# Linear attention on one core: two output stores cut unevenly by partitions, and three more warm-up matmuls

## The chip, the cores and the metric

One Trainium2 chip, one core of it. The time is device microseconds of one execution, the median of several runs; the profile comes from one profiled execution. The cast: TensorE (PE, with its weight loads as PEld), VectorE (DVE), ScalarE (ACT), GpSimd (POOL), and SyncE (SP), which here does nothing but issue transfers. Sixteen DMA engines carry the transfers of the core.

## The reference

Linear attention with the feature map ELU + 1, for B = 1, H = 32 heads, S = 2048 positions, D = 128, all in bf16:

```python
phi_q = jnp.where(q > 0, q + 1, jnp.exp(q)) + 1e-6
phi_k = jnp.where(k > 0, k + 1, jnp.exp(k)) + 1e-6
kv  = jnp.einsum("bhsd,bhse->bhde", phi_k, v)
z   = jnp.einsum("bhsd->bhd", phi_k)
num = jnp.einsum("bhqd,bhde->bhqe", phi_q, kv)
den = jnp.einsum("bhqd,bhd->bhq", phi_q, z)[..., None] + 1e-6
return num / den
```

Each head reads 512 KB each of q, k and v and writes 512 KB. Over 32 heads that is 50.3 MB read and 16.8 MB written.

## The kernel before, in words

The kernel works head by head. A head's 2048 positions lie as 128 partitions of 16 neighbouring positions, so that each partition's part of a tensor is one stretch of 16 x 128 bf16 = 4096 bytes in DRAM (`rows`, L262). The 16 positions of a partition make 16 tiles of 128 x 128.

For each head: the feature map of k is split in two summands, min(exp k, 1) + 1e-6 (`emk_sb`: exponential on ScalarE at L328, the rest on VectorE at L334) and max(k, 0) (`rk_sb`, GpSimd, L330). TensorE sums both against v into a 128 x 128 matrix and a column of sums (`kv`, L342 to L358, into `kvz_ps`). q is transposed on TensorE in two halves of eight tiles (L373, into `x_ps`); its feature map is again two summands, `emq_sb` and `rq_sb` (L384 to L393). Then TensorE computes numerator and denominator in one (L411, L417, into `o_ps`), VectorE adds the epsilon and takes the reciprocal (L456, L460), and VectorE multiplies into `o_sb` (L432, L438); for the last three heads ScalarE takes part of the multiplication (L447).

**The order.** A small planner (`Plan`) holds every operation with its engine and a key; each engine's program is its operations sorted by key, and semaphores are set where an operation needs another engine's result or a free buffer. A key is a position in heads: `h + 0.7` is 0.7 of the way through head h. TensorE's middle heads are a hardware loop; the other engines' programs are written out.

**Transfers.** SP issues all loads (L320) and all stores (L472), in one order by key; only the first head's v is issued by ScalarE (L315). k, q and v have six buffers each (`NBI`), the output has ten (`NBO`). A load is issued when its buffer is free, some six heads ahead. A store of head h has the key h + 1 + 0.18 h (`late`, L476), so that stores fall behind their heads more and more: head 8's stands at 10.44, head 14's at 17.52. Each store is one DMA of 128 partitions by 4096 bytes, except for the last two heads, which are cut by tiles into two and three pieces (`PIECES`, L212). Each output buffer has a semaphore of its own, further pieces get further ones (`EXTRA`); each DMA adds 16 to its semaphore when it has landed. At the end SP waits for all the output semaphores (L149 to L152).

**The warm-up.** Before any data arrives, TensorE runs `warm(9)` (L296): nine matmuls of 128 x 512 on a tile of zeros, into three banks of `o_ps` that nobody reads. The first loads its weights (L288), the other eight keep them (L277).

```python
for n, c in (("k", NBI), ("q", NBI), ("v", NBI), ("o", NBO + 3), ("x", 1)):
    for i in range(c):
        dsems[(n, i)] = es.enter_context(nc.semaphore(f"s_{n}{i}"))
...
late = h + 1.0 + 0.18 * h
for n, (t0, t1) in enumerate(PIECES.get(h, ((0, NT),))):
    store(t0, t1, late + 0.01 * n, bo if n == 0 else NBO + EXTRA[h] + n - 1)
```

Of the kernel before, what the change touches and what calls it, by code (L numbers as in the profile page):

```python
# [11 lines left out]
def _ap(base: bass.AP, elem_offset: int, dims):  # L12
    return bass.AP(base.tensor, base.offset + elem_offset, [list(base.ap[0])] + [list(d) for d in dims])
# [162 lines left out]
def bass_standalone__linear_attn_elu__prompt_kernel(  # L176
# [8 lines left out]
    NT = 16  # L185
# [3 lines left out]
    NBI = 6  # L189
    NBO = 10  # L190
# [20 lines left out]

    PIECES = {NH - 2: ((0, 6), (6, NT)), NH - 1: ((0, 6), (6, 12), (12, NT))}  # L212
    EXTRA = {NH - 2: 0, NH - 1: 1}
    LOOP, TURNS = 3, 4

    qf = q.rearrange("b h s d -> (b h) s d")
# [2 lines left out]
    of = out.rearrange("b h s d -> (b h) s d")  # L219

    with ExitStack() as es:
        def sb(name, shape, dt):
            return es.enter_context(nc.sbuf_tensor(name, shape, dt))
# [14 lines left out]
        o_sb = sb("o_sb", [P, NBO, NT, D], bf16)  # L238
# [11 lines left out]
        def dma_sem(name):  # L250
            return dsems[name]

        for n, c in (("k", NBI), ("q", NBI), ("v", NBI), ("o", NBO + 3), ("x", 1)):
            for i in range(c):
                dsems[(n, i)] = es.enter_context(nc.semaphore(f"s_{n}{i}"))

        block = es.enter_context(nc.Block())
        pl = Plan()

        def rows(x, h):  # L260
            return x[h].rearrange("(p j) d -> p (j d)", j=NT)
# [7 lines left out]
               reads=[("id0",)], writes=[("ident",)])  # L269
# [5 lines left out]
        def mm_held(pe, out, lhsT, rhs, start, stop):  # L275

            return pe.add_instruction(mybir.InstMatmult(  # L277
                name=nc.get_next_instruction_name(), engine=mybir.EngineType.PE, ldweights=False,
                ins=[pe.lower_ap(rhs), pe.lower_ap(lhsT)], outs=[pe.lower_ap(out)], start_tensor_calc=start,
                stop_tensor_calc=stop, tile_size=(P, P), tile_position=(0, 0), bass_skip_group_check=True))  # L280

        def warm(n):

            def f(pe):
                for w in range(n):
                    o = o_ps[:, (2 + w % 3) * 512:(3 + w % 3) * 512]
                    w_sb, zeros = warm_sb[:, :], _ap(warm_sb[:, :], 0, [[0, 4], [1, P]])
                    last = mm_held(pe, o, w_sb, zeros, True, True) if w else pe.matmul(o, lhsT=w_sb, rhs=zeros, start=True, stop=True)  # L288
                return last
            return f  # L290
# [2 lines left out]

        pl.add("act", -9, lambda a: a.activation(rden_sb[:, 0, 0:1], warm_sb[:, 0:1], ACT.Exp), reads=[("warm",)],
               writes=[("rden", 0, 0)])
        pl.add("pe", -9, warm(9), reads=[("warm",)], writes=[("banko", 2), ("banko", 3), ("banko", 4)])  # L296

# [6 lines left out]
        for h in range(NH):  # L306
# [3 lines left out]
            bi, b2, b3, bo = h % NBI, h % 2, h % 3, h % NBO  # L310

            def load(name, buf, src, key, h=h, bi=bi):
# [4 lines left out]
                if name == "v":  # L317
# [11 lines left out]
                   reads=[("k", bi)], writes=[("ek", b2)])  # L329
            pl.add("pool", h, lambda g, bi=bi, b3=b3: g.tensor_scalar(rk_sb[:, b3, :], k_sb[:, bi, :], BIG, 0.0,  # L330
                                                                      op0=ALU.min, op1=ALU.max),
                   reads=[("k", bi)] + ([("emq", 1)] if h == 2 else []), writes=[("rk", b3), ("rkx", b3), ("phik", b3)])
            pl.add("dve", at("emk", -3 + 0.95),
                   lambda d, b2=b2, b3=b3: d.tensor_scalar(emk_sb[:, b3, :], ek_sb[:, b2, :], 1.0, EPS, op0=ALU.min, op1=ALU.add),  # L334
                   reads=[("ek", b2)], writes=[("emk", b3)])

            def added(x, b3=b3):
# [3 lines left out]
                reads=[("emk", b3), ("rkx", b3)] + ([("emq", (h - 1) % 3)] if h else []), writes=[("phik", b3)])  # L341

            def kv(pe, tiles, srcs, h=h, bi=bi, b3=b3):
                for j in tiles:
# [16 lines left out]
                   reads=[("emk", b3), ("rk", b3), ("v", bi), ("ones",), ("vones",)], writes=[("bankkv",)])  # L361
            pl.add("pe", at("kv", -1.2), lambda pe, kv=kv: kv(pe, ADD, (rk_sb,)), reads=[("phik", b3), ("v", bi)], writes=[("bankkv",)])
            pl.add("act", at("kvs", -0.95), lambda a, b3=b3: a.activation(kvs_sb[:, b3, 1:], kvz_ps[:, 1:NC], ACT.Copy),  # L363
                   reads=[("bankkv",)], writes=[("kvs", b3)])
            pl.add("dve", at("zs", -1 + 0.905), lambda d, b3=b3: d.tensor_scalar(  # L365
                kvs_sb[:, b3, 0:1], kvz_ps[:, 0:1], kvz_ps[:, NC:NC + 1], None, op0=ALU.add),
                   reads=[("bankkv",)], writes=[("zs", b3)])
# [14 lines left out]
            for half in (0, 1):  # L382
                pl.add("act", h - 1.1 + 0.05 * half,
                       lambda a, b2=b2, c=cols(half): a.activation(eq_sb[:, b2, c], xT_ps[:, c], ACT.Exp),  # L384
                       reads=[("bankx", half)], writes=[("eq", b2, half)])
            pl.add("act", h - 1.0,
                   lambda a, b3=b3, c=cols(1): a.activation(rq_sb[:, b3, c], xT_ps[:, c], ACT.Relu),  # L387
                   reads=[("bankx", 1)], writes=[("rq", b3, 1)])
            pl.add("dve", at("rq", -2 + 0.948),
                   lambda d, b3=b3, c=cols(0): d.tensor_scalar(rq_sb[:, b3, c], xT_ps[:, c], 0.0, None, op0=ALU.max),  # L390
                   reads=[("bankx", 0)], writes=[("rq", b3, 0)])
            pl.add("dve", at("emq", -2 + 0.955),
                   lambda d, b2=b2, b3=b3: d.tensor_scalar(emq_sb[:, b3, :], eq_sb[:, b2, :], 1.0, EPS, op0=ALU.min, op1=ALU.add),  # L393
                   reads=[("eq", b2, 0), ("eq", b2, 1)], writes=[("emq", b3)])
# [4 lines left out]
            def nbank(b, h=h):  # L399
                return ("bankx", b) if h == NH - 1 and b < 2 else ("banko", b)  # L400
# [20 lines left out]
            for bank in range(NB):  # L421
                pl.add("pe", h + 0.7 + 0.001 * bank, num(bank), reads=phi,
                       writes=[nbank(bank)] + ([nbank(0)] if bank == 1 else []))
# [28 lines left out]
            for g, (b0, b1, place_d, runs) in enumerate(groups):  # L452
# [6 lines left out]
                    reads=banks, writes=[("den", b3, g)])  # L459
                pl.add("dve", key + 0.01, lambda d, b3=b3, b0=b0, b1=b1: d.reciprocal(  # L460
                    rden_sb[:, b3, 4 * b0:4 * b1], den_sb[:, b3, 4 * b0:4 * b1]),
                    reads=[("den", b3, g)], writes=[("rden", b3, g)])
                if g == 0:
                    pl.add("dve", h + 0.911, last_tile, reads=[nbank(0), nbank(1), ("rden", b3, 0)], writes=[("o", bo, NT - 1)])
                for n, (eng, t0, t1, *place_a) in enumerate(runs):
                    pl.add(eng, h + place_a[0] if eng == "act" else key + 0.012 + 0.004 * n,
                           div_act(t0, t1) if eng == "act" else div(t0, t1),
                           reads=[nbank(b) for b in range(t0 // 3, (t1 + 2) // 3)] + [("rden", b3, g)],
                           writes=[("o", bo, t) for t in range(t0, t1)])

            def store(t0, t1, key, slot, h=h, bo=bo):
                pl.add("sp", key, lambda sp: sp.dma_start(rows(of, h)[:, t0 * D:t1 * D],  # L472
                                                          o_sb[:, bo, t0:t1].rearrange("p j d -> p (j d)")),
                       reads=[("o", bo, t) for t in range(t0, t1)], dma=("o", slot))

            late = h + 1.0 + 0.18 * h  # L476
            for n, (t0, t1) in enumerate(PIECES.get(h, ((0, NT),))):
                store(t0, t1, late + 0.01 * n, bo if n == 0 else NBO + EXTRA[h] + n - 1)

# [29 lines left out]
```

## Time and profile before

| what | value |
|---|---|
| time, median of 3 runs (least to most) | 170.68 us (170.59 to 170.80) |
| the profiled execution's own time | 170.68 us |
| its span, first to last instruction | 168.8 us |
| mean granted TensorE clock | 0.994 |
| busy: PE, PEld, DVE, ACT, POOL | 94%, 90%, 89%, 93%, 62% of the span |
| HBM traffic over the span | 398 GB/s |
| a 512 KB load or store, issue to landing (median) | 13.2 to 13.8 us |
| the last store (128 KB), issue to landing | 4.0 us |

The profile is one page, drawn from a trace that can be queried. All its times are counted from the first instruction of the span; the execution's own time is 1.9 us longer than the span. The strip chart cuts the span into 40 slices of 4.2 us; a digit is the busy share in tenths, 9 meaning 90% or more. The chain of waits follows the work that ended last back to the start, each step to what released it. The trace also holds, for each DMA, the times at which its semaphore was raised, 16 times per DMA.

### The profile page before, as it was taken

The page shows a single profiled execution, that of the slowest core. Times are in us where ns is not written, and L with a number is a line of the kernel's source. Part 1 is how long each engine was busy: PE and PEld are TensorE (multiplying, and loading weights), DVE is VectorE, ACT ScalarE, POOL GpSimd, SP SyncE. Part 2 cuts the span into 40 slices and gives each one's busy share as a digit, 9 for nine tenths or more (in the row PEclk, how much of TensorE's full clock was granted, in tenths as well). Part 3 has the DMA queues.
Part 4 walks back from the last instruction along what each step waited for, and adds up shares of the span by engine and source line. Part 5 has one row for each costly group of instructions (what it writes and reads, how often), then busy time and mean ns, then how long its engine had stood idle before and what let it go on. Part 6 is the DMA issues. An engine that isn't in the chain of part 4 may idle for free.

```text
span 168.8 us, 6570 instructions
## 1 busy us (share of the span) xinstructions
PE 158.0 (94%) x3089; PEld 151.7 (90%) x2401; DVE 149.6 (89%) x293; ACT 157.3 (93%) x180; POOL 105.5 (62%) x72
## 2 busy tenths in 40 slices
PE   7588999999999999999999999999999999999940
PEld 0488999999999999999999999999999999999830
DVE  0144999999999999999999999999999999999870
ACT  4599999999999999999999999999999999996960
POOL 3836866666677776666667776666667776666000
PEclk9999999999999999999999999999999999999997
DMA  5999999999999999999999999999999999999982
GB/s 204 412 414 411 412 406 409 406 415 408 411 414 409 415 416 415 418 413 419 415 414 415 416 413 420 413 419 415 413 416 418 417 414 415 411 413 415 412 333 104
DMA packets 22848, 67.31 MB, mean 399 GB/s; under 512 B 2097, under 2 KB 2609, under 8 KB 22833
## 3 DMA queue, kind: packets, MB, share of 16 engines
q1 hardware_dynamic: 22688, 66.59, 98.5%
q10 hardware_dynamic: 144, 0.52, 0.8%
q8 instruction: 9, 0.15, 0.3%
q14 instruction: 7, 0.05, 0.1%
HBM read 50.33 MB, written 16.78 MB: 398 GB/s over the span
## 4 chain that ended last, share of the span: by engine, by line
PE 87%; DMA 3%; DVE 3%; ACT 3%; issue 0%; SPq 0%
PE kvz_ps L355 36%; PE o_ps L411 32%; PE x_ps L373 16%; DMA q_sb<-in_q_dram 3%; DVE o_sb L438 1%; PE o_ps L277 1%; ACT eq_sb L384 1%; PE o_ps L417 1%; PE kvz_ps L277 1%; ACT ek_sb L328 1%; ACT rq_sb L387 1%; DVE emk_sb L334 0%; DVE rden_sb L460 0%; DVE den_sb L456 0%; SPq L320 0%
## 5 line engine op out<-in xcount | busy, mean ns | idle before, releaser
L384 ACT ACTIVATE eq_sb<-x_ps 128x1024 bf16<-128x1024 bf16 x64 | 72.4, 1349 | 3.4 <-PE x_ps L373 3.4
L339 POOL TENSOR_TENSOR rk_sb<-rk_sb,emk_sb 128x640 bf16<-128x640 bf16 x32 | 44.7, 1396 | 47.4 <-DVE emq_sb L393 41.2
L328 ACT ACTIVATE ek_sb<-k_sb 128x2048 bf16<-128x2048 bf16 x32 | 72.2, 2256 | 1.7 <-DMA k_sb<-in_k_dram 1.7
L438 DVE TENSOR_TENSOR o_sb<-o_ps,rden_sb 128x768 bf16<-128x768 f32 (+2 forms) x63 | 68.0, 1119 | 0.1
L355 PE MATMUL kvz_ps<-v_sb,rk_sb 128*128 128x128 bf16 (+1 forms) x512 | 67.6, 218 | 0.0
L330 POOL TENSOR_SCALAR rk_sb<-k_sb 128x2048 bf16<-128x2048 bf16 x32 | 60.6, 1892 | 2.7 <-DMA k_sb<-in_k_dram 2.0
L411 PE MATMUL o_ps<-kvs_sb,emq_sb 128*128 128x129 bf16 x474 | 60.6, 220 | 0.3 <-DVE o_sb L438 0.3
L411 PE MATMUL o_ps<-kvs_sb,rq_sb 128*128 128x129 bf16 x474 | 60.6, 220 | 0.0
L355 PE MATMUL kvz_ps<-v_sb,emk_sb 128*128 128x128 bf16 (+1 forms) x352 | 55.4, 219 | 1.2 <-DVE kvs_sb L365 1.2
L277 PE MATMUL kvz_ps<-ones_sb,rk_sb 128*128 128x1 bf16 x388 | 53.3, 166 | 0.0
L355 PEld LDWEIGHTS kvz_ps<-v_sb,rk_sb 128*128 128x128 bf16 x512 | 47.0, 97 | 1.5
L411 PEld LDWEIGHTS o_ps<-kvs_sb,rq_sb 128*128 128x128 bf16 x474 | 46.2, 97 | 0.0
L411 PEld LDWEIGHTS o_ps<-kvs_sb,emq_sb 128*128 128x128 bf16 x474 | 45.4, 97 | 0.6 <-DVE o_sb L438 0.4
L387 ACT ACTIVATE rq_sb<-x_ps 128x1024 bf16<-128x1024 bf16 x32 | 43.7, 1366 | 0.0
L277 PE MATMUL kvz_ps<-ones_sb,emk_sb 128*128 128x1 bf16 x228 | 37.8, 167 | 0.0
L373 PE MATMUL x_ps<-ident,q_sb 128*128 128x128 bf16 x512 | 34.6, 222 | 1.7 <-DMA q_sb<-in_q_dram 1.7
L373 PEld LDWEIGHTS x_ps<-ident,q_sb 128*128 128x128 bf16 x512 | 30.6, 99 | 5.6 <-DMA q_sb<-in_q_dram 5.6
L355 PEld LDWEIGHTS kvz_ps<-v_sb,emk_sb 128*128 128x128 bf16 x352 | 33.9, 97 | 1.5 <-issue 1.5
L334 DVE TENSOR_SCALAR emk_sb<-ek_sb 128x2048 bf16<-128x2048 bf16 x32 | 21.8, 682 | 8.8 <-ACT ek_sb L328 8.8
L390 DVE TENSOR_SCALAR rq_sb<-x_ps 128x1024 bf16<-128x1024 bf16 x32 | 21.8, 680 | 2.5 <-ACT eq_sb L384 2.5
L393 DVE TENSOR_SCALAR emq_sb<-eq_sb 128x2048 bf16<-128x2048 bf16 x32 | 22.1, 691 | 0.4 <-ACT eq_sb L384 0.4
L363 ACT ACTIVATE kvs_sb<-kvz_ps 128x128 bf16<-128x128 f32 x32 | 20.3, 634 | 0.0
(39 smaller groups left out, 78.2 us busy)
## 6 DMA issues: line engine op xcount, KB each, us to landing
k_sb<-in_k_dram SPq DMA_DIRECT2D x32, 512.0 KB, 13.2
q_sb<-in_q_dram SPq DMA_DIRECT2D x32, 512.0 KB, 13.2
v_sb<-in_v_dram SPq DMA_DIRECT2D x31, 512.0 KB, 13.6
out_dram<-o_sb SPq DMA_DIRECT2D x30, 512.0 KB, 13.8
out_dram<-o_sb SPq DMA_DIRECT2D x3, 192.0 KB, 4.7
v_sb<-in_v_dram ACTq DMA_DIRECT2D x1, 512.0 KB, 4.4
out_dram<-o_sb SPq DMA_DIRECT2D x1, 320.0 KB, 5.6
out_dram<-o_sb SPq DMA_DIRECT2D x1, 128.0 KB, 4.0
```

The lines of the kernel that those rows point to most:

```text
L277: return pe.add_instruction(mybir.InstMatmult(name=nc.get_next_instruction_name(), engine=mybir.EngineType.PE, ldweights=False, ins=[pe.lo ...
L328: lambda a, bi=bi, b2=b2: a.activation(ek_sb[:, b2, :], k_sb[:, bi, :], ACT.Exp),
L330: pl.add("pool", h, lambda g, bi=bi, b3=b3: g.tensor_scalar(rk_sb[:, b3, :], k_sb[:, bi, :], BIG, 0.0, op0=ALU.min, op1=ALU.max), reads=[( ...
L334: lambda d, b2=b2, b3=b3: d.tensor_scalar(emk_sb[:, b3, :], ek_sb[:, b2, :], 1.0, EPS, op0=ALU.min, op1=ALU.add),
L339: pl.add("pool", h + 0.5, lambda g, added=added: g.tensor_tensor(out=added(rk_sb), in0=added(rk_sb), in1=added(emk_sb), op=ALU.add), reads ...
L355: last = pe.matmul(kvz_ps[:, 1 - l:NC + r], lhsT=w, rhs=rhs, start=first, stop=fin, skip_group_check=True)
L373: last = pe.transpose(xT_ps[:, j * P:(j + 1) * P], q_sb[:, bi, j * P:(j + 1) * P], ident[:])
L384: lambda a, b2=b2, c=cols(half): a.activation(eq_sb[:, b2, c], xT_ps[:, c], ACT.Exp),
L387: lambda a, b3=b3, c=cols(1): a.activation(rq_sb[:, b3, c], xT_ps[:, c], ACT.Relu),
L393: lambda d, b2=b2, b3=b3: d.tensor_scalar(emq_sb[:, b3, :], eq_sb[:, b2, :], 1.0, EPS, op0=ALU.min, op1=ALU.add),
L411: last = pe.matmul(o_ap, lhsT=x[:, b3, t * P:(t + 1) * P], rhs=kvs_sb[:, b3, :], start=first, stop=not first)
L438: return lambda d: d.tensor_tensor(out=o_sb[:, bo, t0:t1, :].rearrange("p (a b) d -> p a b d", b=n), in0=_ap(nfull(b), 512 * b + NC * (t0 ...
```

## The change

Two things. The stores of heads 8 and 14 are cut by partitions into three DMAs of 64, 63 and 1 partitions, one after the other in SP's order at the old place (keys `late`, `late + 0.01`, `late + 0.02`); the first keeps the buffer's semaphore, the others get four new ones. Rows and bytes stay as they were. SP issues four DMAs more, and its final wait covers four semaphores more. And the warm-up has twelve matmuls in place of nine. The order of all other instructions on all engines is unchanged.

```diff
+    UNEVEN = {8: (64, 63, 1), 14: (64, 63, 1)}
...
-        for n, c in (("k", NBI), ("q", NBI), ("v", NBI), ("o", NBO + 3), ("x", 1)):
+        for n, c in (("k", NBI), ("q", NBI), ("v", NBI), ("o", NBO + 7), ("x", 1)):
...
-        pl.add("pe", -9, warm(9), reads=[("warm",)], writes=[("banko", 2), ("banko", 3), ("banko", 4)])
+        pl.add("pe", -9, warm(12), reads=[("warm",)], writes=[("banko", 2), ("banko", 3), ("banko", 4)])
...
             late = h + 1.0 + 0.18 * h
+            if h in UNEVEN:
+                r0 = 0
+                for n, r in enumerate(UNEVEN[h]):
+                    pl.add("sp", late + 0.01 * n, lambda sp, h=h, bo=bo, r0=r0, r=r: sp.dma_start(
+                        rows(of, h)[r0:r0 + r, :], o_sb[r0:r0 + r, bo].rearrange("p j d -> p (j d)")),
+                        reads=[("o", bo, t) for t in range(NT)], dma=("o", bo if n == 0 else NBO + 2 + 2 * (h > 8) + n))
+                    r0 += r
+                continue
```

## The prediction, as recorded before the change was run

> **What bounds the kernel now.** I read the page from the top, then its chain of waits, and then, because two of them disagree, the last microseconds by windows and the sixteen completion events that the trace keeps of each transfer.
>
> ```profile
> span 168.8 us, 6570 instructions
> ...
> DMA  5999999999999999999999999999999999999982
> GB/s 204 412 414 411 412 406 409 406 415 408 411 414 409 415 416 415 418 413 419 415 414 415 416 413 420 413 419 415 413 416 418 417 414 415 411 413 415 412 333 104
> ...
> q1 hardware_dynamic: 22688, 66.59, 98.5%
> ...
> PE 87%; DMA 3%; DVE 3%; ACT 3%; issue 0%; SPq 0%
> ```
>
> The chain of waits is 87% TensorE. But the transfers run without a gap from the first slice to the last but two: 412 to 418 GB/s, and 98.5% of sixteen engines' span for SP's queue alone. Two resources are nearly full, so what counts is which of them ends last. The windows of the end tell (columns: stretch, its length, busy time of PE, PEld, DVE, ACT, POOL, granted clock, share of the 16 DMA engines, GB/s):
>
> ```profile
> core 0: us, PE busy (x) PEld busy (x) DVE busy (x) ACT busy (x) POOL busy (x), PEclk, DMA share, GB/s
> 163.00:164.50 1.50, 0.00 (x0) 0.00 (x0) 0.96 (x1) 0.88 (x3) 0.00 (x0) 1.00 0.75 290
> ...
> 165.50:166.00 0.50, 0.00 (x0) 0.00 (x0) 0.00 (x0) 0.00 (x0) 0.00 (x0) 1.00 0.62 222
> 166.00:166.50 0.50, 0.00 (x0) 0.00 (x0) 0.00 (x0) 0.00 (x0) 0.00 (x0) 1.00 0.13 50
> 166.50:167.00 0.50, 0.00 (x0) 0.00 (x0) 0.00 (x0) 0.00 (x0) 0.00 (x0) 0.87 0.11 38
> 167.00:167.60 0.60, 0.00 (x0) 0.00 (x0) 0.00 (x0) 0.00 (x0) 0.00 (x0) 0.50 0.07 25
> 167.60:168.20 0.60, 0.00 (x0) 0.00 (x0) 0.00 (x0) 0.00 (x0) 0.00 (x0) 0.50 0.03 12
> ```
>
> One engine of sixteen is a share of 0.06. From 166 us on two engines are at work, from 167 one. The last store's sixteen completion events say the same: the first fourteen at 166.12 to 166.4 us, the next at 167.24, the last at 168.34; the span ends at 168.82. Through the whole run the distance between the first and the last engine of a transfer grows: 0.24 us at the first load, 2.2 at 33 us, 3.1 at 128, 4.6 at 160. So one engine, which I call the late engine, has been behind all along and never idles; its work alone sets the end. It moves 25 GB/s even when it is alone (the row from 167.00), which is a sixteenth of the full rate: the other engines' rest does not speed it up. TensorE, VectorE and the last issue are some 2 us early for it:
>
> ```profile
> 163.01 0.96 DVE L438 TENSOR_TENSOR o_sb<-o_ps,rden_sb 128x768 bf16<-128x768 f32 x1
> ```
>
> **Price of a row.** 414 GB/s over 16 engines is 25.9 GB/s for one; a partition's row of a store is 4096 bytes, so 0.158 us. The 512 KB store gives each engine 8 of its 128 rows.
>
> **The uneven stores.** Bytes are the same. The 64 rows can go as 4 to each of 16 engines. For the 63 the trace has no example. What it does show in all its 131 DMAs is equal shares: the same number of rows to each engine taking part. 63 rows can be dealt in equal shares to 9, 7, 3 or 1 engines and to no larger number up to 16. The bounds: spread as evenly as can be (15 engines 4 rows, one 3): 0.0 us. All 63 on one engine: 4 + 63 = 67 rows in place of 8, 59 x 0.158 = 9.3 us a head, 18.6 for both. I take equal shares on the most engines, nine with 7 rows each, nearest to what the rows show. Then for each head nine engines get 4 + 7 = 11 rows (3 more), seven get 4 (4 fewer). Over both heads: nine engines +6 x 0.158 = **+0.95 us**, seven engines -8 x 0.158 = **-1.27 us**. The Trainium skill, page "DMA: Bandwidth & Descriptors", section "Why a DMA increments its semaphore by 16 and not by 1", states it as a rule: the largest number up to 16 that divides the slowest dimension, here nine, and always the lowest-numbered engines, so the same nine for both heads. By it the sum is the same; the sixteen events of each 128-row DMA agree with it, and no run here shows 63.
>
> The 1-row piece is one more row on one engine (0.158) or sixteen scraps of 256 bytes (about 0.01 each): 0 to 0.32 us for both; I take 0.03. Two more pieces a head bring each engine up to four completion writes of 6 ns, 0.02 us. The late engine also pays more than its share at stores: there four of its eight rows take 0.17 to 0.18 us, and it falls back about 0.12 us a store. With other rows this may be -0.24 to +0.34 for both heads; I take 0, the middle.
>
> Does it matter that the extra rows come at heads 8 and 14 and not at the end? The issues land 13 us later in the middle of the run, so every engine has a queue and an added row shifts all behind it. The loads can bear a lag of 0.95 us: k of head 31 lands at 145.80 and its exponential begins at 148.75; q lands at 150.98 for 154.7, v at 152.24 for 155.6. The four further issues on SP, and four waits more at its end (L149-152), lie under those 13 us and under the last landing. The ring of ten output buffers leaves head 18 to wait for head 8's last piece, issued 10.4 heads in: eight heads of cover.
>
> **The warm-up.** Three matmuls more of 128x512, on zeros.
>
> ```profile
> 1.39 3.62 PE L277 MATMUL o_ps<-warm_sb 128*128 128x512 bf16 x8
> 6.71 1.89 PE L373 MATMUL x_ps<-ident,q_sb 128*128 128x128 bf16 x16 [1.70 <-DMA q_sb<-in_q_dram]
> ...
> 9.70 0.15 PEld L355 LDWEIGHTS kvz_ps<-v_sb,emk_sb 128*128 128x128 bf16 x1
> 9.84 0.11 PEld L355 LDWEIGHTS kvz_ps<-v_sb,rk_sb 128*128 128x128 bf16 x1
> ```
>
> 3.62/8 = 0.45 each, 1.36 for three, so they end at 5.01 + 1.36 = 6.37, before q lands at 6.71: hidden, with 0.34 us of cover. If q came earlier than that it would cost the difference. They can also give something. Weight loads take 0.15 us up to 9.70 and 0.11 from 9.84: TensorE's clock goes up there. Were it up at 6.71, the first eight transposes (1.05 us on the chain) would take 1.05 x 0.11/0.15 = 0.77. So the gain is 0 to 0.3 us on the TensorE chain, and it ends there: that chain has 2 us to spare against the late engine, whose queue never empties. I count 0. The Trainium skill, page "TensorE: Matmul & The Clock Gate", section "What's actually happening", decides the clock over windows of some 3.4 us; counted back from 9.85 a window is 3.0 to 6.4, which the three matmuls fill, so by it the transposes would be fast; the sum is still 0.
>
> **Sum for the forecast.** Which engines are the nine decides the sign. By count alone the late engine is one of them 9 times in 16. Beside that: packets of different engines that start at one instant stand in the trace in one fixed order, hundreds of times without contradiction, and the late engine is fifth of sixteen. By the Trainium skill (the page and section above) the lowest nine are taken, which would include the fifth if that order is the engines' own; no view here gives an engine a number. So: late engine +0.95 + 0.03 + 0.02 = 1.0 us. It lands at 169.34, the span is 169.8. The profiled execution took 170.68 us, 1.9 beyond its span, and the median is 170.68 too: **171.7 us**, with 171.3 to 172.1 by the unknown terms (-0.4 to +0.4).
>
> **Rivals.**
>
> *Late engine relieved* (faster). If it is one of the seven, it lands at 168.34 - 1.27 = 167.07. The fourteen, nine of them fed 0.95 more, go from 166.4 to 167.35 at most, less what they idle at the end (0.75 of a share in the window from 163.00, so up to 0.4 us). If the second-last engine (167.24) is relieved too, or its late stay goes, the end is at 167.0 to 167.35: -1.0 to -1.3, **169.5 us**. For: 7 in 16. Against: the second-last stands thirteenth in that order, eight places from the late one; in a ring of sixteen, seven neighbours never hold both. But its delay is no store's: a 16 KB instruction fetch (1.1 us at 156.7) made it late, and a few more instructions may put that elsewhere. From the point where the late engine is among the seven, this decides. The Trainium skill, page "DMA: Bandwidth & Descriptors", section "Latency and other measured facts", has engines 7 and 15 as usually the slow ones: 15 would be relieved, 7 loaded.
>
> *Late one relieved, second-last loaded* (same): 167.24 + 0.95 = 168.19, 0.15 earlier: **170.5 us**. The same bin holds the case that the 63 rows are spread evenly and the change doesn't do what it says: 170.7.
>
> *All 63 on one engine* (much slower): +18.6 less the 2 us that an early engine has: about 187. Against it: no DMA of the trace is dealt so.
>
> **How the numbers follow.** Forecast 0.53; relieved 0.29; same 0.15; one engine 0.03. A measurement can tell about 0.2%, 0.34 us, from no change. Slower is 0.53 + 0.03 = 0.56, same 0.15, faster 0.29. The likeliest case's own range is 171.3 to 172.1; both signs hold much, so the range goes from 169.3 to 172.1 and leaves out the one-engine case and edges.
>
> **What would show it.** In the profile after, the landing of a 63-row piece must show nine data-bearing completion events; the late engine's last event minus the fourteen's should stay near 2 us or more for the forecast (all nine go up together) and fall to nothing for the rival. The DMA share after the fourteen end: one engine (0.06) is the forecast, several (0.3 or more) the rival. First transposes at 0.11 us a load, with kv starting at about 13.1 rather than 13.44, and no change at the end, show the warm-up. I am wrong if TensorE's end moves the span, or the late engine has no fixed place between runs.

## The result: 1.09 us slower, and the profile after

The changed kernel takes 171.72 us (median of 6 runs, 171.60 to 172.12), the kernel before 170.63 (170.47 to 170.80) in the same session: a ratio of 1.0067, 95% interval 1.0054 to 1.0080. The forecast was 171.7, on the slower side. The profiled execution took 171.6 us with a span of 169.7.

The page after, the same lines as of before:

```profile
span 169.7 us, 6581 instructions
...
DMA  5999999999999999999999999999999999999980
GB/s 209 406 418 414 406 409 408 390 416 416 405 415 411 416 416 415 418 412 418 415 416 416 416 415 418 415 417 417 416 414 418 417 416 413 413 417 413 405 328 34
...
q1 hardware_dynamic: 22708, 66.59, 98.1%
```

The bytes of SP's queue are the same, 66.59 MB, in 20 more packets, and the slices in the middle are as full as before. The difference is the last slice: 34 GB/s where it was 104. The windows of the end, with the columns of the prediction:

```profile
165.50:166.00 0.50, 0.00 (x0) 0.00 (x0) 0.00 (x0) 0.00 (x0) 0.00 (x0) 0.50 0.33 117
166.00:166.50 0.50, 0.00 (x0) 0.00 (x0) 0.00 (x0) 0.00 (x0) 0.00 (x0) 0.50 0.12 45
166.50:167.00 0.50, 0.00 (x0) 0.00 (x0) 0.00 (x0) 0.00 (x0) 0.00 (x0) 0.50 0.08 32
167.00:167.60 0.60, 0.00 (x0) 0.00 (x0) 0.00 (x0) 0.00 (x0) 0.00 (x0) 0.50 0.06 24
167.60:168.20 0.60, 0.00 (x0) 0.00 (x0) 0.00 (x0) 0.00 (x0) 0.00 (x0) 0.50 0.07 26
168.20:168.80 0.60, 0.00 (x0) 0.00 (x0) 0.00 (x0) 0.00 (x0) 0.00 (x0) 0.50 0.07 25
```

One engine (a share of 0.06 to 0.07) now works alone from 167 to 168.8; before, it was alone from 167.2 and done by 168. The last store's last event comes at 169.26 where it was 168.34, 2.9 us behind the fourteenth where it was 2.0. TensorE and VectorE are not later; their last multiply begins 0.25 us earlier than before:

```profile
162.76 0.96 DVE L439 TENSOR_TENSOR o_sb<-o_ps,rden_sb 128x768 bf16<-128x768 f32 x1
```

How the 63 rows are dealt can be read from the completion events of the pieces of 63 and 1 rows, one list for each DMA, in us:

```
head 8,  63 rows: 74.47 | 83.86 83.97 83.99 84.05 84.53 84.65 85.34 85.35 85.94
head 8,   1 row:  74.86 | 84.15
head 14, 63 rows: 109.83 | 118.29 118.45 118.56 118.91 118.95 119.76 119.78 119.79 121.17
head 14,  1 row:  110.16 | 118.75
```

The first event stands close to the issue, 9 us ahead of the others; a 128-row DMA has sixteen events and all at the landing. So nine engines carry the 63 rows and one carries the single row. The last event, 0.6 and 1.4 us behind the rest, is the late engine's.

How much later the late engine became takes care to read, for ahead of head 8 the last event of a transfer is not its own. It can be told by its habit: its event falls further back at each store, while the others keep their distances. The last four events of some stores, in us behind the store's first event (its landing in the first column); the late engine's are 2.01, 2.14, 2.28 and 2.41 before, 1.84, 3.02 and 3.17 after:

```
before  78.22 | 1.82 2.01 2.13 2.23      after  78.37 | 1.73 1.84 1.88 2.19
before  83.25 | 1.81 2.14 2.17 2.23
before  88.31 | 1.77 2.10 2.20 2.28      after  88.05 | 1.96 2.32 2.33 3.02
before  93.34 | 1.77 2.11 2.20 2.41      after  93.08 | 1.96 2.33 2.34 3.17
```

Ahead of head 8 its event is 0.02 us earlier than before (80.21 and 80.23), behind it 0.48 later (91.07 and 90.59), and at head 14 the difference goes from 0.51 to 1.01: two steps of 0.50, where the prediction had 0.475 for each. One further DMA a head on that engine, at the price of experiment 7, is the rest.

### The profile page after: what moved, and what is told of

It is laid out like the page before. It is cut to its first block, busy times and chain, and to the rows that moved or that the text cites. A ratio compares the mean times of both kernels' runs of the same rounds, so it can differ in the third digit from the quotient of the medians.

```text
span 169.7 us, 6581 instructions
## 1 busy us (share of the span) xinstructions
PE 157.2 (93%) x3092; PEld 150.4 (89%) x2401; DVE 149.9 (88%) x293; ACT 157.4 (93%) x180; POOL 105.6 (62%) x72
## 3 DMA queue, kind: packets, MB, share of 16 engines
q1 hardware_dynamic: 22708, 66.59, 98.1%
## 4 chain that ended last, share of the span: by engine, by line
PE 85%; ACT 5%; DMA 3%; DVE 3%; issue 1%; SPq 0%
PE kvz_ps L356 34%; PE o_ps L412 31%; PE x_ps L374 16%; DMA q_sb<-in_q_dram 3%; ACT eq_sb L385 2%; DVE o_sb L439 1%; PE o_ps L278 1%; ACT ek_sb L329 1%; PE o_ps L418 1%; PE kvz_ps L278 1%; ACT o_sb L448 1%; ACT rq_sb L388 1%; DVE emk_sb L335 0%; DVE rden_sb L461 0%; SPq L321 0%
## 5 line engine op out<-in xcount | busy, mean ns | idle before, releaser
L385 ACT ACTIVATE eq_sb<-x_ps 128x1024 bf16<-128x1024 bf16 x64 | 71.5, 1321 | 3.2 <-PE x_ps L374 3.2
L329 ACT ACTIVATE ek_sb<-k_sb 128x2048 bf16<-128x2048 bf16 x32 | 71.4, 2231 | 1.7 <-DMA k_sb<-in_k_dram 1.7
L356 PE MATMUL kvz_ps<-v_sb,emk_sb 128*128 128x128 bf16 (+1 forms) x352 | 54.8, 218 | 2.2 <-DVE kvs_sb L366 2.1
L388 ACT ACTIVATE rq_sb<-x_ps 128x1024 bf16<-128x1024 bf16 x32 | 42.7, 1334 | 0.0
L374 PE MATMUL x_ps<-ident,q_sb 128*128 128x128 bf16 x512 | 33.8, 219 | 1.2 <-DMA q_sb<-in_q_dram 1.2
L374 PEld LDWEIGHTS x_ps<-ident,q_sb 128*128 128x128 bf16 x512 | 29.9, 98 | 5.7 <-DMA q_sb<-in_q_dram 5.7
L364 ACT ACTIVATE kvs_sb<-kvz_ps 128x128 bf16<-128x128 f32 x32 | 19.2, 599 | 0.0
```

The costliest lines, as they stand in the source:

```text
L329: lambda a, bi=bi, b2=b2: a.activation(ek_sb[:, b2, :], k_sb[:, bi, :], ACT.Exp),
L356: last = pe.matmul(kvz_ps[:, 1 - l:NC + r], lhsT=w, rhs=rhs, start=first, stop=fin, skip_group_check=True)
L374: last = pe.transpose(xT_ps[:, j * P:(j + 1) * P], q_sb[:, bi, j * P:(j + 1) * P], ident[:])
```

## The experiments

The theory: one DMA engine, the fifth, falls behind and never idles; the kernel ends when its rows are done. The rivals: pieces, issues and waits cost by themselves; the TensorE chain counts at the end; the late engine is not at a fixed place. Each comparison is with runs of the kernel before on the same chip (median 170.70). "Outside" is the time less the span; for the kernel before it is 1.87 us. Experiments 3 to 8 have the store loop of the change and the warm-up of nine, with the table of pieces that is shown and a semaphore for each further piece; 9 to 12 are the kernel before with the lines shown.

| kernel | time, us | ratio (95% interval) | span | outside |
|---|---|---|---|---|
| before | 170.70 | | 168.8 | 1.87 |
| warm-up only | 170.79 | 1.0002 (0.9992 to 1.0012) | 168.9 | 1.87 |
| uneven stores only | 171.64 | 1.0049 (1.0035 to 1.0064) | 169.8 | 1.84 |
| 64, 48, 16 | 170.79 | 1.0000 (0.9991 to 1.0009) | 168.9 | 1.87 |
| probe (one run) | 171.86 | | 169.8 | 2.06 |
| 112 and four of 4, three heads | 170.62 | 0.9997 (0.9986 to 1.0009) | 168.4 | 2.27 |
| 112, 5, 5, 5, 1, three heads | 172.07 | 1.0076 (1.0060 to 1.0091) | 169.8 | 2.30 |
| all stores in halves | 171.43 | 1.0043 (1.0027 to 1.0058) | 169.6 | 1.87 |
| 64, 63, 1 in four heads | 172.55 | 1.0106 (1.0089 to 1.0124) | 170.7 | 1.87 |
| four of 4, one semaphore | 170.20 | 0.9972 (0.9962 to 0.9982) | 168.3 | 1.84 |
| 16 rows as 4 x 4 in one DMA | 170.70 | 0.9999 (0.9990 to 1.0007) | 168.8 | 1.86 |
| 24 waits more | 171.33 | 1.0038 (1.0025 to 1.0051) | 169.4 | 1.86 |
| four of 4 in four heads | 171.03 | 1.0015 (1.0003 to 1.0028) | 169.2 | 1.86 |

**1. The warm-up alone.**

```diff
-        pl.add("pe", -9, warm(9), ...
+        pl.add("pe", -9, warm(12), ...
```

> Only the warm-up of twelve matmuls; all stores as before. Theory (one late DMA engine sets the end): VectorE's last multiply ends some 0.25 us earlier, as it does in the changed kernel (163.72 for 163.97), but the last landing stays at about 168.3 us and the time within 0.2% of before, 170.6. Rival (the TensorE chain also counts at the end): the 0.25 us come through, 170.4.

The time is that of before. VectorE did not come earlier here; in this execution its last multiply begins 0.65 us later than before, and the last landing is at 168.32 all the same:

```profile
163.66 0.96 DVE L438 TENSOR_TENSOR o_sb<-o_ps,rden_sb 128x768 bf16<-128x768 f32 x1
```

**2. The uneven stores alone.** The diff of the change without its warm-up line.

> Only the two uneven stores; warm-up of nine. Theory: the whole loss, 0.9 to 1.1 us over before, 171.6 to 171.7, as with the change. Rival (warm-up gains 0.25 us that the stores eat): 171.9 to 172.0.

171.64 us: the loss is all here, with no gain from the warm-up hidden in it. The two kernels with the uneven stores were not timed on one chip, and their ratios (1.0049 and 1.0067) have overlapping intervals.

**3. As many pieces, equal rows.**

```diff
+    UNEVEN = {8: (64, 48, 16), 14: (64, 48, 16)}
```

> Heads 8 and 14 stored in three pieces of 64, 48 and 16 partitions: the same number of DMAs, issues and semaphores as the change, but each engine gets 4 + 3 + 1 = 8 rows as before. Theory (the rows are dealt unequally): no loss, 170.6 to 170.7. Rival (pieces, issues, completion writes or the four waits cost): most of the change's 1.1 us, 171.5 or so.

No change. Four more DMAs, issues, semaphores and waits cost nothing that can be measured; it is the dealing of rows that costs. The same profile shows how little the TensorE chain decides: its last multiply begins 0.66 us earlier than before, the last landing is at 168.24.

```profile
162.35 0.96 DVE L439 TENSOR_TENSOR o_sb<-o_ps,rden_sb 128x768 bf16<-128x768 f32 x1
```

**4. Which engine is late?**

```diff
+    UNEVEN = {4: (112, 3, 13), 7: (112, 4, 12), 10: (112, 5, 11), 13: (112, 6, 10), 16: (112, 7, 9), 19: (112, 8, 8)}
```

> A probe for the late engine's place. Six heads (4, 7, 10, 13, 16, 19) stored as 112, k and 16 - k partitions, k = 3 to 8. If a piece of k rows goes to the k lowest engines with one row each, the late engine (2 us behind) shows as an event that comes some 2 us after the others in the pieces with k above its number, and in none below. If it is number 4, it appears from the piece of 5 on and gets 4 rows more over all (+0.6 us, 171.3); if number 5, from the piece of 6 on, +0.5 us; if it is 9 or higher, in none of the small ones, and it gets fewer rows (170.2 or less). Rival (the nine are not the same each time, or not the lowest): it appears in pieces without such an order.

The completion events of the small pieces (after the first, at the issue):

```
3 rows: 59.34 59.62 59.95
4 rows: 78.39 78.65 78.97 79.19
5 rows: 93.89 94.24 94.25 94.42 96.07
6 rows: 112.94 113.19 113.23 114.15 114.21 115.53
7 rows: 128.17 128.43 128.50 129.19 129.38 129.42 131.19
```

Every piece of k rows has k events. The straggler, 1.3 to 1.8 us behind the next, is absent at 3 and 4 and present from 5 on. So the sets are nested, as far as the straggler tells, and the late engine is the fifth in the order in which they grow: number 4 if they are counted from 0, and not the 7 or 15 that the prediction weighed. The neighbouring pieces say the same. At head 7 the last event of the 112 rows is at 80.34, and one row later, at 80.54, stands the last of the piece of 12; the piece of 4 is done by 79.19. At head 10 the 112 rows end at 95.88, the piece of 5 at 96.07, the piece of 11 at 96.27: one engine's row in each. (The piece of 3 shows little, for at 59 us the late engine was not yet the last.) The Trainium skill ("DMA: Bandwidth & Descriptors", "Why a DMA increments its semaphore by 16 and not by 1") says that the lowest-numbered engines are taken and that the sequencer itself posts the increments of the engines that take no part; the events here agree in their number, with 3 to 13 and with 63 rows on nine; no view gives an engine its number. The single time, 171.86, is above what I expected (171.3): four rows are 0.63 us, and the rest of the 1.2 I can only split in part (the next experiments have a price for a row in a piece of its own, and the time outside the span grew by 0.2).

**5 and 6. Relieve the fifth engine, or load it.** The two kernels have the same number of DMAs and differ in the width of the pieces.

```diff
+    UNEVEN = {h: (112, 4, 4, 4, 4) for h in (8, 14, 20)}
```
```diff
+    UNEVEN = {h: (112, 5, 5, 5, 1) for h in (8, 14, 20)}
```

> Warm-up of nine. Heads 8, 14 and 20 stored as 112 partitions and four pieces of 4: engines 0 to 3 get 11 rows a head, all others 7. Theory (the late engine is the fifth, and its rows set the end): it loses 3 rows, -0.47 us; the first four gain 9 rows, +1.42 us, and end at about 167.8; the second-last is relieved too. Last landing 167.9, time 170.2 us, faster by 0.3%. Rival (any cut store costs time, by its pieces or issues): 171 us or more. Rival (another engine than the fifth): if it is one of the first four, 172.1.

> The same with pieces of 112, 5, 5, 5 and 1: the same number of DMAs, but the fifth engine is now among those loaded: it gets 10 rows a head in place of 8. Theory: +6 rows, +0.95 us, 171.6 to 171.7, so 1.4 us over the kernel with pieces of 4. Rival (the late engine is not the fifth): no difference between the two kernels, within 0.3 us.

Between the two, the span differs by 1.4 us (168.4 and 169.8), which is what 9 rows at 0.158 make (1.42). The sign follows the fifth engine alone. In the profile with pieces of 4, the last event of the common transfers falls against before by 0.19, 0.17 and 0.13 us at the three heads, one row each. But the time did not fall with the span: 170.62 is within noise of before. The span fell by 0.4 us and the time outside it rose by 0.4, as it did in the kernel with pieces of 5. That I had not foreseen; experiments 9 and 11 are about it.

The windows of the kernel with pieces of 5, which show the same engine alone until past 168.8 as in the changed kernel:

```profile
166.50:167.00 0.50, 0.00 (x0) 0.00 (x0) 0.00 (x0) 0.00 (x0) 0.00 (x0) 0.50 0.12 43
167.00:167.60 0.60, 0.00 (x0) 0.00 (x0) 0.00 (x0) 0.00 (x0) 0.00 (x0) 0.50 0.07 26
167.60:168.20 0.60, 0.00 (x0) 0.00 (x0) 0.00 (x0) 0.00 (x0) 0.00 (x0) 0.50 0.06 23
168.20:168.80 0.60, 0.00 (x0) 0.00 (x0) 0.00 (x0) 0.00 (x0) 0.00 (x0) 0.50 0.07 25
```

and of the kernel with pieces of 4, where that stretch is all but empty after 167.6:

```profile
166.50:167.00 0.50, 0.00 (x0) 0.00 (x0) 0.00 (x0) 0.00 (x0) 0.00 (x0) 0.50 0.17 60
167.00:167.60 0.60, 0.00 (x0) 0.00 (x0) 0.00 (x0) 0.00 (x0) 0.00 (x0) 0.50 0.08 28
167.60:168.20 0.60, 0.00 (x0) 0.00 (x0) 0.00 (x0) 0.00 (x0) 0.00 (x0) 0.50 0.01 3
```

The four pieces of a head land on one engine 0.18 to 0.20 us apart (152.53, 152.72, 152.90, 153.10), not 0.158: there a row that is a DMA of its own took some 0.03 us more. The 1.4 us between the two spans do not show that surplus (9 rows at 0.19 would be 1.7).

**7. All stores in halves.**

```diff
+    UNEVEN = {h: (64, 64) for h in range(NH - 2)}
```

> [...] It asks why the late engine is late. Theory (its slowness at stores belongs to the engine): no change, 170.7 to 170.9 (30 completion writes more). Rival (it belongs to the partitions or to the addresses): it is shared with another engine, the late one ends up to 1 us earlier, 169.7 to 170.2.

Neither: 171.43, slower by 0.73 us, 0.024 us for each of the 30 further pieces, which goes with the 0.03 of the experiment before. The lag was not shared out: one engine still falls back alone, 0.06 us at each half (its event is 2.33 us behind the first at 93 us and 3.35 at 141, sixteen halves later). Which partitions an engine carries no view shows, so the experiment does not tell the engine from the partitions or addresses that fall to it. Why the fifth engine is slower at stores stays open.

**8. The dose doubled.**

```diff
+    UNEVEN = {h: (64, 63, 1) for h in (8, 14, 20, 26)}
```

> The dose doubled: heads 8, 14, 20 and 26 stored as 64, 63 and 1, warm-up of nine. Theory (rows on the late engine add up, 3 a head): 12 rows, +1.9 to 2.1 us, 172.6 to 172.8. Rival (a once-only cost of the first cut): 171.7. Rival (the loads come late for the engines, so that the lag also stalls them): more than 173.

172.55 us, +1.85 over before (ratio 1.0106, so +1.5 to +2.1): twice the loss, 12 rows at 0.154.

**9. Pieces of 4 on one semaphore.**

```diff
+            if h in FOUR:
+                r0 = 0
+                for n, r in enumerate((112, 4, 4, 4, 4)):
+                    pl.add("sp", late + 0.01 * n, lambda sp, h=h, bo=bo, r0=r0, r=r: sp.dma_start(
+                        rows(of, h)[r0:r0 + r, :], o_sb[r0:r0 + r, bo].rearrange("p j d -> p (j d)")),
+                        reads=[("o", bo, t) for t in range(NT)], dma=("o", bo))
+                    r0 += r
+                continue
```

> As the kernel with pieces of 112, 4, 4, 4 and 4 in heads 8, 14 and 20, but all five pieces of a head count on the buffer's own semaphore: 12 DMAs more than before and no wait more at SP's end. In the first version the span fell by 0.4 us and the time outside the span rose from 1.87 to 2.27 us. Theory (that rise is an instruction fetch of SP's that falls behind the last landing, since 24 more instructions move the end of its program over a block): with 12 fewer instructions it is gone, span 168.4, outside 1.87, time 170.25 to 170.35, faster by 0.2%. Rival (small pieces themselves lengthen the end of the execution): 170.6 again.

170.20 us, ratio 0.9972 (0.9962 to 0.9982): the fastest version, and faster than both kernels. The time outside the span is 1.84 again. The windows of its end:

```profile
166.00:166.50 0.50, 0.00 (x0) 0.00 (x0) 0.00 (x0) 0.00 (x0) 0.00 (x0) 0.54 0.18 66
166.50:167.00 0.50, 0.00 (x0) 0.00 (x0) 0.00 (x0) 0.00 (x0) 0.00 (x0) 0.50 0.14 50
167.00:167.60 0.60, 0.00 (x0) 0.00 (x0) 0.00 (x0) 0.00 (x0) 0.00 (x0) 0.50 0.04 14
167.60:168.20 0.60, 0.00 (x0) 0.00 (x0) 0.00 (x0) 0.00 (x0) 0.00 (x0) 0.50 0.00 0
```

Three engines share 166 to 166.5, and the last is done before 167.6; the last event is at 167.78, 0.56 us ahead of before, for three rows (0.47).

**10. Sixteen rows, dealt four wide by their shape?** The DRAM side of the last 16 partitions is written as 4 x 4 rows.

```diff
...
+                    rows(of, h)[112:128, :].rearrange("(a b) x -> a b x", b=4),
+                    o_sb[112:128, bo].rearrange("p j d -> p (j d)")),
...
```

> The last 16 partitions of heads 8, 14 and 20 as one DMA whose DRAM side is written as 4 x 4 rows, after one of 112; own semaphore. Theory, if a DMA is dealt by the largest number that divides the slowest dimension of both sides (16 and 4): four engines get 4 rows each, as with four pieces of 4, with 3 DMAs more in place of 12: last landing 0.47 us earlier, 170.2 to 170.3. Rival (only the partitions count, sixteen engines with one row each): 8 rows everywhere, no change, 170.7.

No change, and the piece has sixteen events at its landing. But the shape did not get as far as the chip: the issue stands in the trace with 16 rows in one dimension, as the 128-row stores do with 128. So the theory is not tested here; written this way, 4 x 4 rows are sixteen.

**11. The end of SP's program.**

```diff
+                for i in range(24):
+                    eng.wait_ge(dma_sem(("o", i % 10)), 16 * counts[("o", i % 10)])
```

> The kernel before, its stores and warm-up untouched, with 24 waits more at SP's end, on semaphores that have long been full; nothing else. Theory (the end of SP's program crosses a block of instructions that is fetched after the last landing): span 168.8 as before, time outside the span 2.2 to 2.3 us in place of 1.87, time 171.1. Rival (the rise belongs to the small pieces): 170.7.

171.33 us, but by another way than I expected: the time outside the span is 1.86, and the span is longer by 0.6. The waits stand behind the one for the last landing (168.13, with the span's end at 169.25, 1.1 us later where it is 0.5 before), so each costs 0.025 us by itself. It does not show the fetch of instructions (a transfer of program code) that I looked for. For that theory there remain two rows: the traces of the probe and of the kernel with pieces of 5 hold an 8 KB instruction fetch at 171.5 and 171.9 us, behind the span's end, and their executions took 2.1 and 2.3 us outside the span. The other profiled executions have no such row there, and 1.83 to 1.94 us. The kernel with pieces of 4 is among these, with 1.94: its profile is one of the executions without the 0.4 us, and says nothing for or against. That the 0.4 us go when the pieces share a semaphore is shown; that they are such a fetch goes with the traces and is not shown by an experiment.

**12. Four heads.** As experiment 9, with heads 8, 13, 18 and 23.

> Pieces of 112, 4, 4, 4 and 4 in four heads (8, 13, 18, 23), own semaphore: the late engine loses 4 rows (-0.63 us, landing 167.7), engines 0 to 3 gain 12 (+1.9 us, 166.4 to 168.3 less what they idle at the end, up to 0.4). Theory: the first four now end with or after the late one: span 168.3 to 168.8, time 170.2 to 170.6, no better than three heads. Rival (the first four have more room): 170.1.

171.03 us, slower than three heads by 0.8, and slower than I expected; its times spread over 1.3 us (170.32 to 171.63), those of three heads over 0.45. At the last uneven head four events stand at the end, 0.19 us apart:

```
157.13 157.32 158.48 158.67 158.85 159.04
```

Four landings in a row at that distance are the four small pieces on one engine, and only the first four engines carry them. So one of the first four is now the last: 1.3 us behind the next at the store after (159.97 and 158.69), and 0.85 at the end, at 168.71. At 0.19 us for a small piece the first four gain 4 x 0.19 - 0.158 = 0.6 us a head, 2.4 in four heads, not 1.9. And the four are not equally early: of their events at head 20 in experiment 5 (151.00, 151.53, 151.56, 152.53) the last stands 1.0 us behind the others. In experiment 9, with three heads, the engine just ahead of the last ends 0.4 us before it; it steps back at heads 14 and 20, as only the first four do, and a further head would add more than the 0.4.

This is not the whole of it. Past the last uneven head the event of that engine is 5.6 us behind the first, where it was 3.3 until then, and the two uneven heads before had added only 0.5 and 0.6. A 16 KB instruction fetch (a transfer of program code, which holds one of the sixteen engines) ran just there, 0.97 us from 156.83, and in the kernel before the fetch at 156.72 put an engine back by 1.3 us. No other engine steps back so far here, so in this execution the fetch fell on the engine that was to be last. How much of the 0.8 us is the fetch and how much the fourth head is not settled.

## Why the prediction held, point by point

**What bounds the kernel.** Shown. Over the profiles the last multiply begins between 162.35 and 163.66 us, while the last landing of the kernels that leave the fifth engine its 8 rows a store stays at 168.13 to 168.34 (experiment 7 apart, with thirty further DMAs: 168.87). Rows put on that engine come out at the end one for one (experiments 5, 6 and 8). The chain of waits, 87% TensorE, names an engine with 2 us to spare.

One reading under this head was wrong. The growing distance between the first and the last event is not one engine's: the 2.2 us at 33 us are those of engines that a 16 KB instruction fetch had held. The page has these transfers on queues of their own:

```profile
q8 instruction: 9, 0.15, 0.3%
q14 instruction: 7, 0.05, 0.1%
```

Nine fetches of 16 KB take 0.93 to 1.1 us each in the trace of before (the first at 17.1, 24.0 and 31.5 us), and after each of these three one more engine stands 1.6 us or more behind the first. The late engine is not among them. At the store that lands at 54 us it is 0.73 us behind the first, with seven engines behind it, and only from the store at 88 us on is it the last. What makes it so is 0.12 us at each store and, once, 0.7 us (from 1.16 to 1.89) while an 8 KB fetch ran at 74.8 us. At the end it is the last all the same, and the sum, which went by the end, was right.

**The price and number of rows.** Shown: nine engines, 0.158 us a row. The late engine's steps at the two heads are 0.50 us each for a predicted 0.475; the span grew by 0.9 to 1.0 for a predicted 1.0.

**Which engines.** The forecast had this at 9 in 16, so the sign came out right at odds little over even. The probe settles it: the late engine is the fifth, inside the nine, as the fixed order of the records suggested. The rival with the late engine relieved was the right mechanism with the wrong sign for this change; experiment 9 is that rival made real. The fetch that made the second-last engine late lasts 0.96 us in the trace (at 156.72), not 1.1.

**The small terms.** The completion writes were too low: 6 ns each in the sum, 0.024 us for each further DMA by experiment 7. The late engine takes part in two of the change's four, the pieces of 63, so 0.05 us in place of 0.02. The single row went to one engine, as its one event shows, at some 0.19 us; that engine is not the late one: its event at head 8, 84.15, comes 1.8 us ahead of the late engine's. So 0.03 came out as nothing and 0.02 as 0.05: the two errors cancel, and that the sum is so close is in part luck.

**The late engine's fall at stores.** The 0.12 us a store held: at nine stores from 88 to 133 us its event goes from 2.28 to 3.29 us behind the first. It holds in experiments 1 and 3 too, although the last event of a transfer is there up to 0.5 us later than before between 39 and 110 us: that event is another engine's, 2.7 and 2.5 us back and falling no further, and the late engine passes it at some 117 and 105 us. I took 0 for what other rows would do to this fall, and the two steps of 0.50 us leave no room for more.

**The warm-up.** It is hidden, as said, and 0 at the end. They ended at 5.57 us, not 6.37: the warm-up's matmuls start 0.43 us apart up to 4.38 and 0.21 apart from 4.76, so the clock went up between, within the warm-up. The stretch of kv that was to start at 13.1 us loads its first weights at 13.10, before at 13.40. But "transposes at full clock" is not what the three matmuls decide alone. The first sixteen transposes (columns: start, duration) in the changed kernel and, with nine matmuls, in experiment 2:

```profile
6.82 1.07 PE L374 MATMUL x_ps<-ident,q_sb 128*128 128x128 bf16 x16 [1.25 <-DMA q_sb<-in_q_dram]
```
```profile
6.72 1.07 PE L374 MATMUL x_ps<-ident,q_sb 128*128 128x128 bf16 x16 [1.72 <-DMA q_sb<-in_q_dram]
```

1.07 us both, where the profile of before had 1.89. Of the twelve profiles with nine matmuls, three have the slow transposes (before, experiments 6 and 8); the two with twelve have not. So nine are enough in most executions, which goes with the Trainium skill's clock that is decided over windows not tied to the kernel ("TensorE: Matmul & The Clock Gate", "What's actually happening"); two profiles with twelve are too few to say that twelve always do.

## What to carry to other kernels

When sixteen DMA engines are nearly full, do not stop at their mean: look at the distance between the first and the last completion event of one transfer as it grows through the run, and at which engine holds the last: follow one engine by what it loses where, for the last at a fifth of the run need not be the last at its end. A store's partition count decides on which engines its rows land, so rows can be moved off a late engine as well as on to it; here three rows were worth 0.5 us, once the pieces shared one semaphore. Before loading others, ask what the earliest of them can take, and count a further DMA at what the trace shows for one.

## What the runs showed of the hardware that I had not expected

- A further DMA costs its engines something besides its rows: 0.024 us each where all sixteen carry it (experiment 7), and rows sent as DMAs of their own land 0.19 us apart where 0.158 is the price in a large store.
- The fifth engine falls back by 0.12 us at each 512 KB store, in the four kernels in which I followed it (before and experiments 1, 3 and 7, there 0.06 at each half), and not at loads; its last landing is steady to 0.2 us over kernels in which other engines differ by 0.5 us in the middle.
- A 16 KB instruction fetch holds one DMA engine for 0.9 to 1.1 us and puts it back by more than that (1.3 us for the one at 156.72 in the kernel before); it moves the end when that engine is to be the last (experiment 12).
- Each wait on a semaphore that is already full costs SP 0.025 us, once it stands behind the last landing; ahead of it such waits cost nothing (experiment 3 has four, experiment 5 twelve, and 0.48 us from the last landing to the span's end as before).
- The time outside the span is not a constant: 1.84 to 1.89 us for most kernels, 2.27 and 2.30 for the two with twelve further DMAs on twelve further semaphores, 2.06 in the one run of the probe, which has as many, but 1.87 with thirty (experiment 7).
